# Decode attention over two caches: 64 KB rows per partition, products written over K, fewer buffers

## The chip, the cores and the metric

One core of one Trainium2 chip. The metric is device time in microseconds (us), the median of several executions.

The words used for the units of the core: VectorE (DVE in the profile), TensorE (PE), ScalarE (ACT), SyncE (SP, which here only issues transfers), and the 16 DMA engines, which move data from HBM, the chip's main memory, to SBUF, the core's own memory of 128 partitions.

## The reference

Two independent one-token attention layers, A and B, each with 32 heads of width 128. A attends to all 16384 keys of its cache, B to the last 4096.

```python
q = (x @ wq).reshape(B, Sq, Hq, Dh).transpose(0, 2, 1, 3)
# A: k, v = k_cache, v_cache                      (32 heads x 16384 keys x 128)
# B: k, v = k_cache[:, :, Sk - 4096:, :], ...     (32 heads x  4096 keys x 128)
scores = einsum("bhqd,bhkd->bhqk", q, k) * Dh ** -0.5
o = einsum("bhqk,bhkd->bhqd", softmax(scores), v)
out = concat([oA.reshape(B, Sq, Hq * Dh) @ woA, oB.reshape(B, Sq, Hq * Dh) @ woB])
```

K and V that are read: 32 x 16384 x 128 x 2 bytes x 2 for A, a quarter of that for B; with the projections 352.3 MB in all. Each key is used once, so this is a kernel about moving 352 MB.

## The kernel before

A unit is one 4 MB K load and one 4 MB V load: one head of A, or four heads of B. A partition gets one contiguous row of 32 KB. For A, partition p has keys 128p to 128p+127. For B, the four heads are interleaved: partition 4i+g has the i-th row of head g.

```python
def _load_kv(nc, cx, unit, which):
    # ... (pool, tile [P, unit.keys = 128, DH])
    n = len(unit.heads)                                   # 1 for A, 4 for B
    src = view[unit.heads[0] : unit.heads[0] + n].rearrange("g (i l) d -> i g l d", i=P // n)
    cx.o(nc.sync.dma_start(out=t[:, :, :], in_=src[:, 0, :, :] if n == 1 else src))

def _mult(nc, cx, ch):          # chunk of U = 64 keys a partition
    ch.prod = cx.prod_pool.tile([P, U, DH], BF16, tag="prod", name="prod")
    # ... prod = K chunk * q (broadcast)                  VectorE
def _add(nc, cx, ch):
    # ... half = prod[:, :, :64] + prod[:, :, 64:]        VectorE
# _red: TensorE sums half to red; _softmax: VectorE sums red to sc, ScalarE exp
# _pv: TensorE multiplies p and V, accumulating over the four heads of a group
cx.kt_pool = pool("kt", 2); cx.vt_pool = pool("vt", 2)    # two K and two V buffers
```

Where heads are interleaved, the query block holds each partition's own head's q, and exp gets a bias of -1000 on the partitions of the other heads.

The softmax here doesn't subtract the row's maximum and nothing guards it: scores larger than these inputs give would overflow.

Of the kernel before, what the change touches and what calls it, by code (L numbers as in the profile page):

```python
# [10 lines left out]
P = 128  # L11
# [5 lines left out]
G = 4  # L17
U = 64
SCALE = 1.0 / math.sqrt(DH)
# [21 lines left out]
class _Loads:  # L41



    def __init__(self):
        self.todo, self.free = [], {}
# [16 lines left out]
class _Group:  # L63


    def __init__(self, st, i):
        self.st, self.i, self.heads = st, i, list(range(i * G, (i + 1) * G))
        self.acc = self.cs = None


class _Chunk:


    def __init__(self, unit, i):
        self.unit, self.i, self.k0 = unit, i, i * U
        self.last_of_unit = self.k0 + U == unit.keys


class _Unit:
    kt = vt = None  # L80


def _load_x(nc, cx, st):

    D = st.wq.shape[0]
    KC = D // P
    xT = cx.singles.tile([P, KC], BF16, tag=f"xT{st.name}", name=f"xT{st.name}")
    nc.scalar.dma_start(out=xT[:, :], in_=st.x[0, 0, :].rearrange("(p c) -> p c", c=KC))
    R = st.mix
    st.xb = cx.singles.tile([P, KC, R, P], BF16, tag=f"xb{st.name}", name=f"xb{st.name}")  # L90
    if R > 1:
        cx.o(nc.vector.memset(st.xb[:, :, :, :], 0.0))
    for g in range(R):
        for c in range(KC):
            cx.o(nc.vector.tensor_copy(  # L95
                st.xb[:, c, g, :].rearrange("p (i r) -> p r i", r=R)[:, g, :],
                xT[:, c : c + 1].broadcast_to([P, P // R]),
            ))


def _load_wq(nc, cx, st, tag):
    D, N = st.wq.shape
    KC = D // P
    st.wq_tag = tag
    pool = cx.kt_pool if tag == "kt" else cx.vt_pool
    st.wq_t = pool.tile([P, KC, N], BF16, tag=tag, name="wq_t")
    cx.o(nc.sync.dma_start(out=st.wq_t[:, :, :], in_=st.wq.rearrange("(p c) f -> p c f", c=KC)))  # L107


def _q(nc, cx, st):  # L110


    D, N = st.wq.shape
    KC = D // P
    R = st.mix
# [15 lines left out]
    cx.loads.release(st.wq_tag)  # L131


def _load_wo(nc, cx, st, j0, n):


    J = st.wo.shape[0] // P
    if j0 == 0:
        st.wo_t = cx.kt_pool.tile([P, J, st.DN], BF16, tag="kt", name=f"wo{st.name}")
    src = st.wo.rearrange("(p j) f -> p j f", j=J)  # L140
    cx.o(nc.sync.dma_start(out=st.wo_t[:, j0 : j0 + n, :], in_=src[:, j0 : j0 + n, :]))  # L141

# [37 lines left out]
def _red(nc, cx, ch):  # L180
# [3 lines left out]
    for b in range(nb):  # L184
# [11 lines left out]


# [365 lines left out]
```

## Time and profile before

| kernel before | value |
|---|---|
| time | 829.09 us (829.01 to 829.31, 3 runs) |
| DMA queue busy, share of 16 engines' span | 99.1% |
| VectorE / TensorE busy | 71% / 49% |
| bytes read | 352.3 MB, 426 GB/s over the span |

The page of the kernel before: the DMA's share of each of 40 slices of the span in tenths, and the rate in each; the packets; the load queue; the chain of waits, by engine and by line; four groups of instructions (count, busy us, mean ns, idle time before them and what ended it); and the K and V loads (size, median us from issue to landing).

```profile
DMA  9999999999999999999999999999999999999996
GB/s 380 434 430 432 432 432 435 431 432 430 434 429 434 430 431 430 434 431 426 434 432 430 429 431 430 431 432 432 432 430 431 429 431 433 431 433 431 432 423 285
DMA packets 13133, 352.68 MB, mean 426 GB/s; under 512 B 1714, under 2 KB 1716, under 8 KB 2100
...
q1 hardware_dynamic: 12820, 352.33, 99.1%
...
DMA 69%; DVE 20%; issue 10%; SPq 0%; DVEq 0%; PE 0%
DMA kt<-in_A_k_cache_dram 53%; DMA kt<-in_B_k_cache_dram 13%; DVE prod L160 12%; DVE half L172 6%; DMA woB<-in_B_wo_dram 3%; DVE sc L202 2%; SPq L141 0%; DVE recip L266 0%; DVEq L160 0%; PE out L302 0%; SPq L107 0%; DVE rowB L311 0%
...
L160 DVE TENSOR_TENSOR prod<-kt,qallA 128x8192 bf16<-128x8192 bf16 x64 | 283.3, 4426 | 159.8 <-DMA kt<-in_A_k_cache_dram 159.1
L172 DVE TENSOR_TENSOR half<-prod 128x4096 bf16<-128x4096 bf16 x80 | 182.6, 2282 | 0.0
...
L160 DVE TENSOR_TENSOR prod<-kt,qallB 128x8192 bf16<-128x8192 bf16 x16 | 70.8, 4426 | 40.2 <-DMA kt<-in_B_k_cache_dram 39.9
L232 PE MATMUL acc<-vt,pA 128*16 128x512 bf16 x1024 | 87.2, 474 | 2.0 <-DMA vt<-in_A_v_cache_dram 2.0
...
kt<-in_A_k_cache_dram SPq DMA_DIRECT2D x32, 4096.0 KB, 27.0
vt<-in_A_v_cache_dram SPq DMA_DIRECT2D x32, 4096.0 KB, 29.6
kt<-in_B_k_cache_dram SPq DMA_DIRECT2D x8, 4096.0 KB, 27.0
vt<-in_B_v_cache_dram SPq DMA_DIRECT2D x8, 4096.0 KB, 29.6
```

Two windows of the kernel before (busy us of each engine, then the granted clock, the DMA's share and its rate).

```profile
core 0: us, PE busy (x) PEld busy (x) DVE busy (x) ACT busy (x) POOL busy (x), PEclk, DMA share, GB/s
160.55:199.41 38.86, 17.04 (x96) 5.43 (x96) 28.91 (x13) 1.40 (x8) 0.00 (x0) 0.69 1.00 431
199.41:238.27 38.86, 20.14 (x124) 7.31 (x124) 28.96 (x14) 5.10 (x23) 0.00 (x0) 0.69 1.01 432
```

Read together: the load queue hardly pauses (busy 99.1%), a 4 MB load that needs 9.7 us at 432 GB/s lands 27 to 30 us after its issue, so it queues behind two others, and VectorE works 29 of each 38.9 us. The chain names VectorE because it frees the buffers (SP waits 428.9 us in all for the product in L160), but by then other loads are already queued. The trace also has a record of every DMA packet; a row of 32 KB is one packet:

```
row bytes      4096   8192   16384   32768     (kernel before, lowest busy ns of a packet)
busy ns         159    309     611    1213
```

That is 36.75 ns per 1000 bytes (37.6 ns per KB as the row lengths count it, 1024 bytes) and some 9 ns for each packet. The prediction's "36.75 ns per KB" is the first of these. A load ends with 16 records of 4 bytes, its completion records, of 9 ns each (median). The kernel before also has 18 instruction packets of 16 KB, which took 1.02 to 1.10 us where the lowest for that size is 0.61. At three of them (55, 427 and 795 us) the spread between the first and the last completion record of a load rose by 1.1 to 1.5 us, from 0.5 to 4.9 us in all.

### The profile page before, as it was taken

The page shows a single profiled execution, that of the slowest core. Times are in us where ns is not written, and L with a number is a line of the kernel's source. Part 1 is how long each engine was busy: PE and PEld are TensorE (multiplying, and loading weights), DVE is VectorE, ACT ScalarE, POOL GpSimd, SP SyncE. Part 2 cuts the span into 40 slices and gives each one's busy share as a digit, 9 for nine tenths or more (in the row PEclk, how much of TensorE's full clock was granted, in tenths as well). Part 3 has the DMA queues.
Part 4 walks back from the last instruction along what each step waited for, and adds up shares of the span by engine and source line. Part 5 has one row for each costly group of instructions (what it writes and reads, how often), then busy time and mean ns, then how long its engine had stood idle before and what let it go on. Part 6 is the DMA issues. An engine that isn't in the chain of part 4 may idle for free.

```text
span 827.4 us, 5697 instructions
## 1 busy us (share of the span) xinstructions
PE 402.1 (49%) x2368; PEld 139.4 (17%) x2368; DVE 584.8 (71%) x286; ACT 68.2 (8%) x301; POOL 4.6 (1%) x17
## 2 busy tenths in 40 slices
PE   3356434434554535544454445545455345464355
PEld 1112111111211112211121111111112111121123
DVE  2892777777777777766777777777777776777760
ACT  2000011000100001000110001100010000100010
POOL 2000000000000000000000000000000000000000
PEclk9778687666676676776677676666676766766778
DMA  9999999999999999999999999999999999999996
GB/s 380 434 430 432 432 432 435 431 432 430 434 429 434 430 431 430 434 431 426 434 432 430 429 431 430 431 432 432 432 430 431 429 431 433 431 433 431 432 423 285
DMA packets 13133, 352.68 MB, mean 426 GB/s; under 512 B 1714, under 2 KB 1716, under 8 KB 2100
## 3 DMA queue, kind: packets, MB, share of 16 engines
q1 hardware_dynamic: 12820, 352.33, 99.1%
q8 instruction: 18, 0.29, 0.1%
q10 hardware_dynamic: 288, 0.00, 0.0%
q14 instruction: 7, 0.06, 0.0%
HBM read 352.32 MB, written 0.00 MB: 426 GB/s over the span
## 4 chain that ended last, share of the span: by engine, by line
DMA 69%; DVE 20%; issue 10%; SPq 0%; DVEq 0%; PE 0%
DMA kt<-in_A_k_cache_dram 53%; DMA kt<-in_B_k_cache_dram 13%; DVE prod L160 12%; DVE half L172 6%; DMA woB<-in_B_wo_dram 3%; DVE sc L202 2%; SPq L141 0%; DVE recip L266 0%; DVEq L160 0%; PE out L302 0%; SPq L107 0%; DVE rowB L311 0%
## 5 line engine op out<-in xcount | busy, mean ns | idle before, releaser
L185 PE MATMUL red<-half,ident 128*128 128x512 bf16 x640 | 252.4, 566 | 388.7 <-DVE half L172 388.7
L160 DVE TENSOR_TENSOR prod<-kt,qallA 128x8192 bf16<-128x8192 bf16 x64 | 283.3, 4426 | 159.8 <-DMA kt<-in_A_k_cache_dram 159.1
L172 DVE TENSOR_TENSOR half<-prod 128x4096 bf16<-128x4096 bf16 x80 | 182.6, 2282 | 0.0
L185 PEld LDWEIGHTS <-ident 128*128 128x128 bf16 x640 | 81.9, 128 | 534.0 <-issue 506.2
L160 DVE TENSOR_TENSOR prod<-kt,qallB 128x8192 bf16<-128x8192 bf16 x16 | 70.8, 4426 | 40.2 <-DMA kt<-in_B_k_cache_dram 39.9
L232 PE MATMUL acc<-vt,pA 128*16 128x512 bf16 x1024 | 87.2, 474 | 2.0 <-DMA vt<-in_A_v_cache_dram 2.0
L209 ACT ACTIVATE pA<-sc 128x64 bf16<-128x64 f32 x64 | 16.4, 256 | 512.2 <-DVE sc L202 512.2
L202 DVE TENSOR_REDUCE sc<-red 128x64 f32<-128x512 f32 x80 | 54.8, 684 | 3.7 <-PE red L185 3.6
L232 PEld LDWEIGHTS <-pA 128*16 128x16 bf16 x1024 | 22.5, 99 | 72.6 <-issue 65.2
L209 ACT ACTIVATE p_sb<-sc,off 128x64 bf16<-128x64 f32 x64 | 21.5, 336 | 91.4 <-DVE sc L202 91.4
L256 PE MATMUL f_ps<-acc_sb,sel 128*4 128x128 f32 x128 | 16.6, 273 | 10.7 <-ACT acc_sb L243 10.7
L232 PE MATMUL acc<-vt,p_sb 128*16 128x512 bf16 x256 | 21.3, 464 | 0.0
L243 ACT COPY acc_sb<-acc 128x512 f32<-128x512 f32 x16 | 9.4, 586 | 85.6 <-PE acc L232 85.6
L123 PE MATMUL q_ps<-wq_t,xbA 128*128 128x512 bf16 x32 | 8.7, 439 | 13.1 <-DMA wq_t<-in_A_wq_dram 13.1
L256 PEld LDWEIGHTS f_ps<-acc_sb,sel 128*4 128x4 f32 x128 | 9.8, 86 | 14.5 <-ACT acc_sb L243 12.3
L209 ACT ACTIVATION_READ_ACCUMULATOR pA<-sc 128x1 f32 x64 | 11.9, 187 | 0.0
L209 ACT ACTIVATION_READ_ACCUMULATOR p_sb<-sc,off 128x1 f32 x64 | 11.9, 186 | 0.0
L232 PEld LDWEIGHTS <-p_sb 128*16 128x16 bf16 x256 | 5.6, 97 | 16.3 <-issue 14.1
L123 PE MATMUL q_ps<-wq_t,xbB 128*128 128x512 bf16 x32 | 7.2, 378 | 2.0 <-DMA wq_t<-in_B_wq_dram 1.3
L268 ACT ACTIVATE orow<-f_ps,recip 4x128 bf16<-4x128 f32 x16 | 5.7, 358 | 20.5 <-DVE recip L266 20.5
L95 DVE COPY xbB<-xTB 128x32 bf16<-128x32 bf16 x16 | 1.5, 197 | 8.1 <-DMA xTB<-in_B_x_dram 8.1
L266 DVE RECIPROCAL recip<-f_ps 4x1 f32<-4x1 f32 x16 | 2.4, 150 | 5.8 <-PE f_ps L256 5.8
(35 smaller groups left out, 54.8 us busy)
## 6 DMA issues: line engine op xcount, KB each, us to landing
kt<-in_A_k_cache_dram SPq DMA_DIRECT2D x32, 4096.0 KB, 27.0
vt<-in_A_v_cache_dram SPq DMA_DIRECT2D x32, 4096.0 KB, 29.6
kt<-in_B_k_cache_dram SPq DMA_DIRECT2D x8, 4096.0 KB, 27.0
vt<-in_B_v_cache_dram SPq DMA_DIRECT2D x8, 4096.0 KB, 29.6
wq_t<-in_A_wq_dram SPq DMA_DIRECT2D x1, 4096.0 KB, 12.3
wq_t<-in_B_wq_dram SPq DMA_DIRECT2D x1, 4096.0 KB, 24.1
woA<-in_A_wo_dram SPq DMA_DIRECT2D x2, 2048.0 KB, 31.3
woB<-in_B_wo_dram SPq DMA_DIRECT2D x1, 2048.0 KB, 23.8
```

What stands on the lines that cost most here:

```text
L95: cx.o(nc.vector.tensor_copy(st.xb[:, c, g, :].rearrange("p (i r) -> p r i", r=R)[:, g, :], xT[:, c : c + 1].broadcast_to([P, P // R]),))
L123: cx.o(nc.tensor.matmul(q_ps[:, :], lhsT=st.xb[:, c, g, :], rhs=w[:, g, j * (512 // DH) : (j + 1) * (512 // DH), :], start=(g == 0 and c = ...
L160: cx.o(nc.vector.tensor_tensor(out=ch.prod[:, :, :], in0=u.kt[:, ch.k0 : ch.k0 + U, :], in1=q.rearrange("p (o d) -> p o d", o=1).broadcast ...
L172: cx.o(nc.vector.tensor_tensor(out=ch.half[:, :, :], in0=ch.prod[:, :, 0 : DH // 2], in1=ch.prod[:, :, DH // 2 : DH], op=ALU.add,))
L185: cx.o(nc.tensor.matmul(ch.red[:, :, :], lhsT=cx.ident[:, :], rhs=ch.half[:, :, b * W : (b + 1) * W], start=(b == 0), stop=(b == nb - 1),))
L202: cx.o(nc.vector.tensor_reduce(out=sc[:, :], in_=ch.red[:, :, :], axis=AX.X, op=ALU.add))
L209: cx.o(nc.scalar.activation(out=ch.p[:, :, g, :], in_=sc[:, :].rearrange("p (t e) -> p t e", e=4), func=ACT.Exp, scale=SCALE, bias=0.0 if ...
L232: cx.o(nc.tensor.matmul(gr.acc[r : r + 4 * G, :], lhsT=ch.p[:, t, :, :], rhs=u.vt[:, k : k + 4, :], start=(first and t < 4), stop=(last an ...
L243: cx.o(nc.scalar.copy(gr.acc_sb[:, :], gr.acc[:, :]))
L256: cx.o(nc.tensor.matmul(gr.f_ps[:, 0:DH], lhsT=cx.sel[:, e, :], rhs=gr.acc_sb[:, e * DH : (e + 1) * DH], start=False, stop=(e == 3), skip_ ...
L266: cx.o(nc.vector.reciprocal(recip[:, :], gr.f_ps[:, DH : DH + 1]))
L268: cx.o(nc.scalar.activation(out=gr.orow[:, :], in_=gr.f_ps[:, 0:DH], func=ACT.Copy, scale=recip[:, 0:1]))
```

## The change

Its intent: the same bytes in half as many loads with rows twice as long, to lose fewer fixed costs in the stream that bounds the kernel. A unit is now 8 MB of K and 8 MB of V, 64 KB a partition: two heads of A (partition 2i+g) or eight of B (partition 8i+g). To make room, q*k and the half sums are written over K, there are two K buffers and one V buffer, and each unit has its own accumulator.

```diff
-G = 4
+KEYS = 256
 def _load_kv(...):
-    n = len(unit.heads)
-    src = view[unit.heads[0] : unit.heads[0] + n].rearrange("g (i l) d -> i g l d", i=P // n)
-    cx.o(nc.sync.dma_start(out=t[:, :, :], in_=src[:, 0, :, :] if n == 1 else src))
+    src = view[unit.h0 : unit.h0 + unit.R].rearrange("g (i l) d -> i g l d", l=KEYS)
+    cx.o(nc.sync.dma_start(out=t[:, :, :], in_=src))          # R = 2 for A, 8 for B
 def _mult(...):
-        out=ch.prod[:, :, :], in0=u.kt[:, ch.k0 : ch.k0 + U, :],
+        out=k, in0=k,                                          # k = the K chunk itself
 def _add(...):
-        out=ch.half[:, :, :], in0=ch.prod[:, :, 0:64], in1=ch.prod[:, :, 64:128],
+        out=k[:, :, 0:64], in0=k[:, :, 0:64], in1=k[:, :, 64:128],
-    cx.vt_pool = pool("vt", 2)
+    cx.vt_pool = pool("vt", 1)
     # ... (P.V of a whole unit in one go, during the next unit; projections first;
     #      the last V goes to a K buffer; cut)
```

The shape in which a load names its source, slowest dimension first:

```
             before                      changed
A    128 rows x 32 KB             64 x 2 rows x 64 KB
B    32 x 4 rows x 32 KB          16 x 8 rows x 64 KB
```

More of the change, by code (lines that the diff above doesn't have):

```diff
@@ L41, with __init__ @@
 class _Loads:
-    def __init__(self):
-        self.todo, self.free = [], {}
+    def __init__(self, free):
+        self.todo, self.free = [], free
     def add(self, pool, fn):
@@ L60, in pump @@
             fn()
-class _Group:
-    def __init__(self, st, i):
-        self.st, self.i, self.heads = st, i, list(range(i * G, (i + 1) * G))
-        self.acc = self.cs = None
 class _Chunk:
@@ L75, in __init__, with _load_x, _load_wq @@
         self.unit, self.i, self.k0 = unit, i, i * U
-        self.last_of_unit = self.k0 + U == unit.keys
 class _Unit:
-    kt = vt = None
-def _load_x(nc, cx, st):
+    def __init__(self, st, i):
+        self.st, self.i, self.R = st, i, st.R
+        self.h0 = i * st.R
+        self.chunks = [_Chunk(self, c) for c in range(KEYS // U)]
+        self.stage = None
+def _load_x(nc, cx, st, at):
     D = st.wq.shape[0]
     KC = D // P
+    R = st.R
     xT = cx.singles.tile([P, KC], BF16, tag=f"xT{st.name}", name=f"xT{st.name}")
     nc.scalar.dma_start(out=xT[:, :], in_=st.x[0, 0, :].rearrange("(p c) -> p c", c=KC))
-    R = st.mix
-    st.xb = cx.singles.tile([P, KC, R, P], BF16, tag=f"xb{st.name}", name=f"xb{st.name}")
-    if R > 1:
-        cx.o(nc.vector.memset(st.xb[:, :, :, :], 0.0))
+    n = KC * R * P
+    st.xb = cx.scr[:, at : at + n].rearrange("p (c g m) -> p c g m", c=KC, g=R)
+    cx.o(nc.vector.memset(cx.scr[:, at : at + n], 0.0))
     for g in range(R):
-        for c in range(KC):
-            cx.o(nc.vector.tensor_copy(
-                st.xb[:, c, g, :].rearrange("p (i r) -> p r i", r=R)[:, g, :],
-                xT[:, c : c + 1].broadcast_to([P, P // R]),
-            ))
-def _load_wq(nc, cx, st, tag):
+        cx.o(nc.vector.tensor_copy(
+            st.xb[:, :, g, :].rearrange("p c (i r) -> p r c i", r=R)[:, g, :, :],
+            xT[:, :].rearrange("p (c o) -> p c o", o=1).broadcast_to([P, KC, P // R]),
+        ))
+    return at + n
+def _load_wq(nc, cx, st, w):
     D, N = st.wq.shape
     KC = D // P
-    st.wq_tag = tag
-    pool = cx.kt_pool if tag == "kt" else cx.vt_pool
-    st.wq_t = pool.tile([P, KC, N], BF16, tag=tag, name="wq_t")
-    cx.o(nc.sync.dma_start(out=st.wq_t[:, :, :], in_=st.wq.rearrange("(p c) f -> p c f", c=KC)))
+    if w == 0:
+        cx.wq_t = cx.vt_pool.tile([P, 2, KC, N], BF16, tag="vt", name="wq_t")
+    st.wq_t = cx.wq_t[:, w, :, :]
+    cx.o(nc.sync.dma_start(out=st.wq_t, in_=st.wq.rearrange("(p c) f -> p c f", c=KC)))
 def _q(nc, cx, st):
@@ L114, in _q @@
     KC = D // P
-    R = st.mix
+    R = st.R
     n = N // R
@@ L130, in _q, with _load_kv @@
         cx.o(nc.scalar.copy(st.qall[:, j * 512 : (j + 1) * 512], q_ps[:, :]))
-    cx.loads.release(st.wq_tag)
 def _load_wo(nc, cx, st, j0, n):
     J = st.wo.shape[0] // P
-    if j0 == 0:
-        st.wo_t = cx.kt_pool.tile([P, J, st.DN], BF16, tag="kt", name=f"wo{st.name}")
+    if cx.wo_t is None:
+        cx.wo_t = cx.vt_pool.tile([P, 2, J, st.DN], BF16, tag="vt", name="wo_t")
     src = st.wo.rearrange("(p j) f -> p j f", j=J)
+    st.wo_t = cx.wo_t[:, st.at // st.DN, :, :]
     cx.o(nc.sync.dma_start(out=st.wo_t[:, j0 : j0 + n, :], in_=src[:, j0 : j0 + n, :]))
-def _load_kv(nc, cx, unit, which):
-    pool, tag = (cx.kt_pool, "kt") if which == "k" else (cx.vt_pool, "vt")
-    t = pool.tile([P, unit.keys, DH], BF16, tag=tag, name=tag)
-    setattr(unit, tag, t)
+def _load_kv(nc, cx, unit, which, tag):
+    pool = cx.kt_pool if tag == "kt" else cx.vt_pool
+    t = pool.tile([P, KEYS, DH], BF16, tag=tag, name=which)
+    setattr(unit, which, t)
+    unit.v_tag = tag
     st = unit.st
-    view = st.k_view if which == "k" else st.v_view
-    n = len(unit.heads)
-    src = view[unit.heads[0] : unit.heads[0] + n].rearrange("g (i l) d -> i g l d", i=P // n)
-    cx.o(nc.sync.dma_start(out=t[:, :, :], in_=src[:, 0, :, :] if n == 1 else src))
+    view = st.k_view if which == "kt" else st.v_view
+    src = view[unit.h0 : unit.h0 + unit.R].rearrange("g (i l) d -> i g l d", l=KEYS)
+    cx.o(nc.sync.dma_start(out=t[:, :, :], in_=src))
 def _mult(nc, cx, ch):
     u = ch.unit
-    ch.prod = cx.prod_pool.tile([P, U, DH], BF16, tag="prod", name="prod")
-    q = u.st.qall[:, u.q_at * DH : (u.q_at + 1) * DH]
+    k = u.kt[:, ch.k0 : ch.k0 + U, :]
+    q = u.st.qall[:, u.i * DH : (u.i + 1) * DH]
     cx.o(nc.vector.tensor_tensor(
-        out=ch.prod[:, :, :],
-        in0=u.kt[:, ch.k0 : ch.k0 + U, :],
+        out=k, in0=k,
         in1=q.rearrange("p (o d) -> p o d", o=1).broadcast_to([P, U, DH]),
@@ L165, in _mult @@
     ))
-    if ch.last_of_unit:
-        cx.loads.release("kt")
 def _add(nc, cx, ch):
-    ch.half = cx.half_pool.tile([P, U, DH // 2], BF16, tag="half", name="half")
+    k = ch.unit.kt[:, ch.k0 : ch.k0 + U, :]
     cx.o(nc.vector.tensor_tensor(
-        out=ch.half[:, :, :],
-        in0=ch.prod[:, :, 0 : DH // 2],
-        in1=ch.prod[:, :, DH // 2 : DH],
-        op=ALU.add,
+        out=k[:, :, 0 : DH // 2], in0=k[:, :, 0 : DH // 2], in1=k[:, :, DH // 2 : DH], op=ALU.add,
     ))
@@ L187, in _red @@
             lhsT=cx.ident[:, :],
-            rhs=ch.half[:, :, b * W : (b + 1) * W],
+            rhs=ch.unit.kt[:, ch.k0 : ch.k0 + U, b * W : (b + 1) * W],
             start=(b == 0),
@@ L191, in _red @@
         ))
+    if ch.k0 + U == KEYS:
+        cx.loads.release("kt")
 def _softmax(nc, cx, ch):
-    u, gr = ch.unit, ch.unit.group
-    if gr.cs is None:
-        gr.cs = cx.cs_pool.tile([P, 2, G], F32, tag=f"cs{gr.st.name}", name="cs")
-    sc = cx.small.tile([P, U], F32, tag="sc", name="sc")
-    cx.o(nc.vector.tensor_reduce(out=sc[:, :], in_=ch.red[:, :, :], axis=AX.X, op=ALU.add))
-    if len(u.heads) == 1:
-        ch.p = cx.pA[u.heads[0] % G][ch.i]
-    else:
-        ch.p = cx.p_pool.tile([P, U // 4, G, 4], BF16, tag="p", name="p_sb")
-    for h in u.heads:
-        g = h % G
+    u = ch.unit
+    R = u.R
+    if ch.i == 0:
+        u.cs = cx.cs_pool.tile([P, KEYS // U, R], F32, tag=f"cs{u.st.name}", name="cs")
+    sc = cx.sc_pool.tile([P, U], F32, tag="sc", name="sc")
+    cx.o(nc.vector.tensor_reduce(out=sc[:, :], in_=ch.red[:, :, :], axis=AX.X, op=ALU.add))
+    ch.p = u.st.p_pool.tile([P, U // 4, R, 4], BF16, tag=f"p{u.st.name}", name="p_sb")
+    for g in range(R):
         cx.o(nc.scalar.activation(
@@ L213, in _softmax @@
             scale=SCALE,
-            bias=0.0 if len(u.heads) == 1 else cx.off[:, g : g + 1],
-            accum_out=gr.cs[:, ch.i, g : g + 1],
-        ))
-def _pv(nc, cx, ch):
-    u, gr = ch.unit, ch.unit.group
-    first = u.heads[0] == gr.heads[0] and ch.i == 0
-    last = u.heads[-1] == gr.heads[-1] and ch.last_of_unit
-    if first:
-        cx.turn = 1 - cx.turn
-        gr.acc = cx.acc[cx.turn]
-    T = U // 4
+            bias=u.st.off[:, g : g + 1],
+            accum_out=u.cs[:, ch.i, g : g + 1],
+        ))
@@ L229, in _pv @@
+def _pv(nc, cx, u):
+    R = u.R
+    u.csum = cx.small.tile([P, R], F32, tag=f"csum{u.st.name}", name="csum")
+    cx.o(nc.vector.tensor_reduce(
+        out=u.csum[:, :], in_=u.cs[:, :, :].rearrange("p i g -> p g i"), axis=AX.X, op=ALU.add,
+    ))
+    cx.turn = 1 - cx.turn
+    acc = cx.acc[cx.turn]
+    T = KEYS // 4
     for t in range(T):
         r = 32 * (t % 4)
-        k = ch.k0 + 4 * t
+        ch = u.chunks[4 * t // U]
         cx.o(nc.tensor.matmul(
-            gr.acc[r : r + 4 * G, :],
-            lhsT=ch.p[:, t, :, :],
-            rhs=u.vt[:, k : k + 4, :],
-            start=(first and t < 4),
-            stop=(last and t >= T - 4),
-        ))
@@ L239, in _pv @@
-    if ch.last_of_unit:
-        cx.loads.release("vt")
-    if last:
-        gr.acc_sb = cx.accs_pool.tile([P, 4 * DH], F32, tag="accs", name="acc_sb")
-        cx.o(nc.scalar.copy(gr.acc_sb[:, :], gr.acc[:, :]))
-    return gr if last else None
-def _fin_fold(nc, cx, gr):
-    gr.f_ps = cx.psf_pool.tile([G, DH + 1], F32, tag="f", name="f_ps")
-    for i in range(2):
-        cx.o(nc.tensor.matmul(
-            gr.f_ps[:, DH : DH + 1], lhsT=gr.cs[:, i, :], rhs=cx.ones_col[:, 0:1],
-            start=(i == 0), stop=(i == 1), skip_group_check=True,
-        ))
+            acc[r : r + 4 * R, :],
@@ new lines, in _pv, with _fin_fold @@
+            lhsT=ch.p[:, t % (U // 4), :, :],
+            rhs=u.vt[:, 4 * t : 4 * t + 4, :],
+            start=(t < 4),
+            stop=(t >= T - 4),
+        ))
+    cx.loads.release(u.v_tag)
+    u.acc_sb = cx.accs_pool.tile([P, 4 * DH], F32, tag="accs", name="acc_sb")
+    cx.o(nc.scalar.copy(u.acc_sb[:, :], acc[:, :]))
+def _fin_fold(nc, cx, u):
+    R = u.R
+    u.f_ps = cx.psf_pool.tile([8, DH + 1], F32, tag="f", name="f_ps")
+    cx.o(nc.tensor.matmul(
+        u.f_ps[0:R, DH : DH + 1], lhsT=u.csum[:, :], rhs=cx.ones_col[:, 0:1],
+        start=True, stop=True, skip_group_check=True,
+    ))
@@ L255, in _fin_fold, with _fin_row @@
     for e in range(4):
         cx.o(nc.tensor.matmul(
-            gr.f_ps[:, 0:DH],
-            lhsT=cx.sel[:, e, :],
-            rhs=gr.acc_sb[:, e * DH : (e + 1) * DH],
+            u.f_ps[0:R, 0:DH],
+            lhsT=cx.sel[:, e, 0:R],
+            rhs=u.acc_sb[:, e * DH : (e + 1) * DH],
             start=False, stop=(e == 3), skip_group_check=True,
         ))
-def _fin_row(nc, cx, gr):
-    recip = cx.small.tile([G, 1], F32, tag="recip", name="recip")
-    cx.o(nc.vector.reciprocal(recip[:, :], gr.f_ps[:, DH : DH + 1]))
-    gr.orow = cx.small.tile([G, DH], BF16, tag="orow", name="orow")
+def _fin_row(nc, cx, u):
+    R = u.R
+    recip = cx.small.tile([8, 1], F32, tag="recip", name="recip")
+    cx.o(nc.vector.reciprocal(recip[0:R, :], u.f_ps[0:R, DH : DH + 1]))
+    u.orow = cx.small.tile([8, DH], BF16, tag="orow", name="orow")
@@ L268, in _fin_row, with _fin_col @@
     cx.o(nc.scalar.activation(
-        out=gr.orow[:, :], in_=gr.f_ps[:, 0:DH], func=ACT.Copy, scale=recip[:, 0:1]
+        out=u.orow[0:R, :], in_=u.f_ps[0:R, 0:DH], func=ACT.Copy, scale=recip[0:R, 0:1]
     ))
-def _fin_col(nc, cx, gr):
-    st = gr.st
+def _fin_col(nc, cx, u):
+    st = u.st
     J = st.wo.shape[0] // P
-    R = DH // J
-    at = (len(st.groups) - 1 - gr.i) * G * R
-    for r in range(R):
+    n = DH // J
+    last = u.i == len(st.units) - 1
+    for r in range(n):
+        at = cx.place_at - n * u.h0 - r
@@ L281, in _fin_col @@
         cx.o(nc.tensor.matmul(
             cx.oc_ps[:, st.oc_at : st.oc_at + J],
-            lhsT=cx.place[0:G, r, at : at + P],
-            rhs=gr.orow[:, r * J : (r + 1) * J],
-            start=(cx.oc_first and r == 0), stop=(gr.i == len(st.groups) - 1 and r == R - 1),
+            lhsT=cx.place[0 : u.R, at : at + P],
+            rhs=u.orow[0 : u.R, r * J : (r + 1) * J],
+            start=(cx.oc_first and r == 0), stop=(last and r == n - 1),
             skip_group_check=True,
@@ L309, in _out @@
     if j0 + n == J:
-        row = cx.singles.tile([1, st.DN], BF16, tag=f"row{st.name}", name=f"row{st.name}")
+        row = cx.accs_pool.tile([1, st.DN], BF16, tag="accs", name=f"row{st.name}")
         cx.o(nc.vector.tensor_copy(row[0:1, 0:w], out[0]))
@@ L342 @@
     cx.singles = pool("singles", 1)
-    cx.small = pool("small", 4)
+    cx.small = pool("small", 1)
     cx.kt_pool = pool("kt", 2)
-    cx.vt_pool = pool("vt", 2)
-    cx.prod_pool = pool("prod", 1)
-    cx.half_pool = pool("half", 2)
-    cx.accs_pool = pool("accs", 2)
+    cx.vt_pool = pool("vt", 1)
+    cx.accs_pool = pool("accs", 1)
     cx.cs_pool = pool("cs", 2)
-    cx.p_pool = pool("p", 4)
+    cx.sc_pool = pool("sc", 2)
+    cx.p_poolA = pool("pA", 8)
+    cx.p_poolB = pool("pB", 4)
     cx.red_pool = pool("red", 2, **PS)
@@ L354, with problem @@
     cx.psout_pool = pool("psout", 1, **PS)
-    ld = cx.loads = _Loads()
-    ld.free = {"kt": 2, "vt": 2}
+    ld = cx.loads = _Loads({"kt": 1, "vt": 1})
+    cx.scr = cx.kt_pool.tile([P, KEYS * DH], BF16, tag="kt", name="scr")
+    cx.wo_t = None
+    def problem(name, x, k_cache, v_cache, wq, wo, sk0, W, at):
+        st = _Problem()
+        st.name, st.x, st.wq, st.wo, st.at = name, x, wq, wo, at
+        st.R = P * KEYS // W
+        st.DN = wo.shape[1]
+        st.k_view = k_cache[0, :, sk0 : sk0 + W, :]
+        st.v_view = v_cache[0, :, sk0 : sk0 + W, :]
+        st.oc_at, st.out_rows = (0, (0, 32)) if name == "A" else (64, (64, 96))
+        st.p_pool = cx.p_poolA if name == "A" else cx.p_poolB
+        st.units = [_Unit(st, i) for i in range(k_cache.shape[1] // st.R)]
+        return st
+    stA = problem("A", A_x, A_k_cache, A_v_cache, A_wq, A_wo, 0, SkA, 0)
+    stB = problem("B", B_x, B_k_cache, B_v_cache, B_wq, B_wo, SkB - WB, WB, A_wo.shape[1])
+    units = []
+    per = len(stA.units) // len(stB.units)
+    for i, u in enumerate(stA.units):
+        units.append(u)
+        if i % per == per - 1:
+            units.append(stB.units[i // per])
+    n = len(units)
+    ld.add("vt", lambda: _load_wq(nc, cx, stA, 0))
+    ld.add(None, lambda: _load_wq(nc, cx, stB, 1))
+    for i, u in enumerate(units):
+        ld.add("kt", lambda u=u: _load_kv(nc, cx, u, "kt", "kt"))
+        if i:
+            ld.add("vt", lambda u=units[i - 1]: _load_kv(nc, cx, u, "vt", "vt"))
+    ld.add("kt", lambda u=units[-1]: _load_kv(nc, cx, u, "vt", "kt"))
+    J = A_wo.shape[0] // P
+    pieces = [(stA, 0, J // 2), (stA, J // 2, J // 2)]
+    j0 = 0
+    for x in (J // 2, J // 4, J // 8, J // 16, J // 16):
+        pieces.append((stB, j0, x))
+        j0 += x
+    for i, p in enumerate(pieces):
+        ld.add(None if i else "vt", lambda p=p: _load_wo(nc, cx, *p))
+    ld.pump()
+    at = _load_x(nc, cx, stA, 0)
+    at = _load_x(nc, cx, stB, at)
     cx.ones_col = cx.singles.tile([P, 1], F32, tag="ones_col", name="ones_col")
     nc.gpsimd.memset(cx.ones_col[:, :], 1.0)
-    ones_mat = cx.singles.tile([P, P], BF16, tag="ones_mat", name="ones_mat")
-    nc.gpsimd.memset(ones_mat[:, :], 1.0)
+    ones = cx.scr[:, at : at + 2 * P]
+    nc.gpsimd.memset(ones, 1.0)
     cx.ident = cx.singles.tile([P, P], BF16, tag="ident", name="ident")
@@ L364 @@
         out=cx.ident[:, :],
-        in_=ones_mat[:, :],
+        in_=ones[:, 0:P],
         pattern=[[-1, P]],
@@ L371 @@
     )
-    cx.sel = cx.singles.tile([P, 4, G], F32, tag="sel", name="sel")
+    n_r = DH // J
+    cx.place_at = n_r * (stA.units[-1].h0) + n_r - 1
+    w = cx.place_at + P
+    cx.place = cx.singles.tile([8, 2 * P], BF16, tag="place", name="place")
+    nc.gpsimd.affine_select(
+        out=cx.place[:, 0:w],
+        in_=ones[0:8, 0:w],
+        pattern=[[1, w]],
+        compare_op=ALU.is_equal,
+        fill=0.0,
+        base=-cx.place_at,
+        channel_multiplier=-n_r,
+    )
+    cx.sel = cx.singles.tile([P, 4, 8], F32, tag="sel", name="sel")
     nc.vector.tensor_reduce(
         out=cx.sel[:, :, :].rearrange("p e g -> p g e"),
-        in_=cx.ident[:, :].rearrange("p (t g e) -> p g e t", t=4, g=8)[:, 0:G, :, :],
+        in_=cx.ident[:, :].rearrange("p (t g e) -> p g e t", t=4, g=8),
         axis=AX.X,
@@ L381 @@
     )
-    cx.off = cx.singles.tile([P, G], F32, tag="off", name="off")
-    nc.vector.tensor_reduce(
-        out=cx.off[:, :],
-        in_=cx.ident[:, :].rearrange("p (i g) -> p g i", g=G),
-        axis=AX.X,
-        op=ALU.add,
-    )
-    nc.vector.tensor_scalar(
-        out=cx.off[:, :], in0=cx.off[:, :], scalar1=-1.0, scalar2=1000.0,
-        op0=ALU.add, op1=ALU.mult,
-    )
-    J = A_wo.shape[0] // P
-    R = DH // J
-    w = 2 * P - G * R
-    ones_row = cx.singles.tile([G, R * w], BF16, tag="ones_row", name="ones_row")
-    nc.gpsimd.memset(ones_row[:, :], 1.0)
-    cx.place = cx.singles.tile([G, R, w], BF16, tag="place", name="place")
-    nc.gpsimd.affine_select(
-        out=cx.place[:, :, :],
-        in_=ones_row[:, :].rearrange("p (r c) -> p r c", r=R),
-        pattern=[[-1, R], [1, w]],
-        compare_op=ALU.is_equal,
-        fill=0.0,
-        base=-(P - G * R),
-        channel_multiplier=-R,
-    )
-    cx.pA = []
-    for g in range(G):
-        cx.pA.append([])
-        for i in range(2):
-            t = cx.singles.tile([P, U // 4, G, 4], BF16, tag=f"pA{g}{i}", name=f"pA{g}{i}")
-            nc.gpsimd.memset(t[:, :, :, :], 0.0)
-            cx.pA[g].append(t)
+    for st in (stA, stB):
+        st.off = cx.singles.tile([P, st.R], F32, tag=f"off{st.name}", name=f"off{st.name}")
+        nc.vector.tensor_reduce(
+            out=st.off[:, :],
+            in_=cx.ident[:, :].rearrange("p (i g) -> p g i", g=st.R),
+            axis=AX.X,
+            op=ALU.add,
+        )
+        nc.vector.tensor_scalar(
+            out=st.off[:, :], in0=st.off[:, :], scalar1=-1.0, scalar2=1000.0,
+            op0=ALU.add, op1=ALU.mult,
+        )
     cx.turn = 0
@@ L427 @@
     ]
-    def problem(name, x, k_cache, v_cache, wq, wo, sk0, W, at):
-        st = _Problem()
-        st.name, st.x, st.wq, st.wo, st.W, st.at = name, x, wq, wo, W, at
-        st.H = k_cache.shape[1]
-        st.DN = wo.shape[1]
-        st.k_view = k_cache[0, :, sk0 : sk0 + W, :]
-        st.v_view = v_cache[0, :, sk0 : sk0 + W, :]
-        st.oc_at, st.out_rows = (0, (0, 32)) if name == "A" else (64, (64, 96))
-        st.mix = 1 if W == SkA else G
-        st.groups = [_Group(st, i) for i in range(st.H // G)]
-        return st
@@ L441 @@
-    stA = problem("A", A_x, A_k_cache, A_v_cache, A_wq, A_wo, 0, SkA, 0)
-    stB = problem("B", B_x, B_k_cache, B_v_cache, B_wq, B_wo, SkB - WB, WB, A_wo.shape[1])
-    units = []
-    for h in range(stA.H):
-        units.append((stA, [h]))
-        if h % G == G - 1:
-            units.append((stB, list(range(h - G + 1, h + 1))))
-    chunks = []
-    for i, (st, heads) in enumerate(units):
-        u = units[i] = _Unit()
-        u.st, u.heads, u.group = st, heads, st.groups[heads[0] // G]
-        u.keys = st.W * len(heads) // P
-        u.q_at = heads[0] // len(heads)
-        u.chunks = [_Chunk(u, i) for i in range(u.keys // U)]
-        chunks += u.chunks
@@ L460 @@
-    ld.add("vt", lambda: _load_wq(nc, cx, stA, "vt"))
-    n = len(units)
-    for i in range(n + 1):
-        if i == G - 1:
-            ld.add("kt", lambda: _load_wq(nc, cx, stB, "kt"))
-        if i < n:
-            ld.add("kt", lambda u=units[i]: _load_kv(nc, cx, u, "k"))
-        if i:
-            ld.add("vt", lambda u=units[i - 1]: _load_kv(nc, cx, u, "v"))
-    pieces = [(stA, 0, J // 2), (stA, J // 2, J // 2)]
-    j0 = 0
-    for x in (J // 2, J // 4, J // 8, J // 16, J // 16):
-        pieces.append((stB, j0, x))
-        j0 += x
@@ L474 @@
-    for p in pieces:
-        ld.add(None if p[1] else "kt", lambda p=p: _load_wo(nc, cx, *p))
-    _load_x(nc, cx, stA)
-    _load_x(nc, cx, stB)
-    ld.pump()
     _q(nc, cx, stA)
+    _q(nc, cx, stB)
+    ld.release("kt")
+    ld.release("vt")
     fins = []
     def fin_pe():
-        for gr in fins:
-            if gr.stage == 0:
-                _fin_fold(nc, cx, gr)
-                gr.stage = 1
-            elif gr.stage == 2:
-                _fin_col(nc, cx, gr)
-                gr.stage = 9
-        fins[:] = [gr for gr in fins if gr.stage != 9]
@@ L494, in fin_dve @@
-    def fin_dve():
-        for gr in fins:
-            if gr.stage == 1:
-                _fin_row(nc, cx, gr)
-                gr.stage = 2
-    def pv(ch):
-        gr = _pv(nc, cx, ch)
-        if gr is not None:
-            gr.stage = 0
-            fins.append(gr)
-    prev = None
-    waiting = []
-    for c, ch in enumerate(chunks):
-        if c == 2 * (G - 1):
-            _q(nc, cx, stB)
-        _mult(nc, cx, ch)
-        if prev is not None:
-            _softmax(nc, cx, prev)
-            waiting.append(prev)
-        fin_pe()
-        _add(nc, cx, ch)
-        fin_dve()
-        _red(nc, cx, ch)
-        if len(waiting) > 1:
-            pv(waiting.pop(0))
-        prev = ch
@@ L522 @@
-    _softmax(nc, cx, prev)
-    waiting.append(prev)
-    for ch in waiting:
-        fin_pe()
-        fin_dve()
-        pv(ch)
+        for u in fins:
+            if u.stage == 0:
+                _fin_fold(nc, cx, u)
+                u.stage = 1
+            elif u.stage == 2:
+                _fin_col(nc, cx, u)
+                u.stage = 9
+        fins[:] = [u for u in fins if u.stage != 9]
+    def fin_dve():
+        for u in fins:
+            if u.stage == 1:
+                _fin_row(nc, cx, u)
+                u.stage = 2
@@ new lines, in pv @@
+    def pv(u):
+        _pv(nc, cx, u)
+        u.stage = 0
+        fins.append(u)
+    prev = None
+    for i, u in enumerate(units):
+        for ch in u.chunks:
+            _mult(nc, cx, ch)
+            if prev is not None:
+                _softmax(nc, cx, prev)
+            fin_pe()
+            _add(nc, cx, ch)
+            fin_dve()
+            _red(nc, cx, ch)
+            if i and ch.i == min(i - 1, 2):
+                pv(units[i - 1])
+            prev = ch
+    _softmax(nc, cx, prev)
@@ L528 @@
+    fin_pe()
+    fin_dve()
+    pv(units[-1])
     while fins:
```

## The prediction

> **What bounds it now.** The DMA queue. The page shows the load queue busy 99.1% of 16 engines' span; steady windows of 38.86 us move 430 to 432 GB/s[...]. VectorE is busy 71%, TensorE 49%. The chain of waits is 69% DMA; its VectorE pieces only say when a buffer came free. The issue list shows 27 to 30 us from issue to landing for loads that need 9.7 us: two are always queued behind the running one. The 352.3 MB stay.
>
> [...] The DMA packet records give busy time by size: 4 KB 159 ns, 8 KB 309, 16 KB 611, 32 KB 1213 (lowest values; the 32 KB mean is 1218). That is a line: 36.75 ns per KB plus about 9 ns. Each completion record of a load[...] takes another 9 ns. The rest is outside the stream: 2.8 us before the first row, 18 instruction fetches of 16 KB on the same engines, which let the slowest engine lag the fastest by 0.5 us early, 3.4 later, 4.9 near the end, and 3 us after the last landing.
>
> **What the change removes.** K/V rows grow from 32 to 64 KB: 640 row packets an engine become 320, saving 320 x 9 ns = 2.9 us (estimate from the line above); 80 K/V loads become 40, saving 0.4 us of completion records. All of it is on the critical path. Sum 3.2 us, if a 64 KB row stays one packet. [...] no trace here shows it yet. If rows are cut in two, only 0.4 us is left.
>
> **What it adds or moves.** In-place multiply and add have the same shapes (4.43 and 2.28 us); score sums 0.68. A unit of four chunks needs 4 x 7.4 = 29.5 us of VectorE against 38.9 us for its 16.8 MB. Exps grow on ScalarE (for B about 4.2 us a chunk), far from limiting. With one V buffer, the next V is issued after the previous unit's P.V: K lands at t, three chunks 22 us, reduction 3.5, 64 P.V matmuls 4.2 to 5.5 us (16 took 1.04 to 1.09): t+31, against t+38.9 when the queue would run dry: slack 8 us. K is released near t+36, needed at t+58. First compute begins at 41 us instead of 23, costless because V and wo follow the last K anyway. Projections end by 32 us, before K0 lands. Tail: 10 us of wo-A covers the last P.V and fold.
>
> **Prediction.** 826.1 us; 80% range 824.4 to 829.3. Faster by over 2%: 0.01; within 2%: 0.96; slower: 0.03.
>
> **What would show it.** About 5120 row packets of 65,536 B at about 2420 ns, no idle stretch in the DMA slices, 432 to 434 GB/s, landing to landing of K about 38.7 us; SP's wait for P.V ending 7 us or more before the running K load lands; tail unchanged; VectorE instruction times unchanged.
>
> **What would make it wrong.** 64 KB rows cut in two (about 828.7); instruction fetches falling on one engine (up to 1.5 us each); the V slack vanishing because P.V or VectorE slows, idling the queue each unit (20 us per us of shortfall); a late K1; strided in-place operands slowing VectorE over 30%.

The forecast's sum: 320 x 9 ns for row packets and 40 x 9 ns for completion records, 3.2 us. Where the second paragraph has 2.8 us before the first row, the packet records have the first 16 rows start 2.0 to 2.9 us into the span.

## The result, and the profile after

| | before | changed |
|---|---|---|
| time, us | 829.12 (4 runs) | 1052.85 (1045.08 to 1054.47, 4 runs) |
| ratio | | 1.268, 95% interval 1.264 to 1.272 |
| DMA rate over the span, GB/s | 426 | 335 |
| VectorE busy, us | 584.8 | 584.2 |

A ratio is the mean time of one kernel's runs over that of the other's of the same rounds, so not quite the ratio of the medians. The changed kernel is 27% slower where 0.4% faster was predicted.

The page of the changed kernel, the same parts as before:

```profile
DMA  9999999999999999999999999997999999999970
GB/s 399 439 437 439 435 429 208 282 437 214 267 437 430 434 434 227 252 435 244 242 420 424 410 429 287 203 421 260 202 344 405 404 437 399 200 299 244 193 286 32
DMA packets 7375, 352.70 MB, mean 335 GB/s; under 512 B 1074, under 2 KB 1076, under 8 KB 1460
...
q1 hardware_dynamic: 7060, 352.33, 95.7%
...
DMA 33%; another core or an unknown queue 23%; DVE 23%; PE 14%; issue 7%; ACT 1%; SPq 0%; ACTq 0%; DVEq 0%
DMA kt<-in_A_k_cache_dram 21%; DVE kt L151 11%; DVE kt L160 9%; DMA vt<-in_A_v_cache_dram 7%; PE acc L214 7%; PE red L170 5%; DMA wo_t<-in_B_wo_dram 5%; DVE sc L188 3%; PE f_ps L234 1%; ACT acc_sb L223 1%; PE out L279 0%; DVE recip L245 0%; SPq L132 0%; SPq L101 0%
...
L151 DVE TENSOR_TENSOR kt<-kt,qallA 128x8192 bf16<-128x8192 bf16 x64 | 282.8, 4419 | 147.8 <-DMA kt<-in_A_k_cache_dram 147.8
L160 DVE TENSOR_TENSOR kt<-kt 128x4096 bf16<-128x4096 bf16 x80 | 182.6, 2283 | 0.0
...
L151 DVE TENSOR_TENSOR kt<-kt,qallB 128x8192 bf16<-128x8192 bf16 x16 | 70.7, 4421 | 129.2 <-DMA kt<-in_B_k_cache_dram 129.2
L214 PE MATMUL acc<-vt,p_sb 128*8 128x512 bf16 (+1 forms) x1280 | 97.2, 471 | 98.8 <-DMA vt<-in_B_v_cache_dram 75.6
```

Its K and V loads, from the view of DMA issues (8 MB each):

```profile
kt<-in_A_k_cache_dram SPq DMA_DIRECT2D x16, 47.6
vt<-in_A_v_cache_dram SPq DMA_DIRECT2D x16, 36.7
kt<-in_B_k_cache_dram SPq DMA_DIRECT2D x4, 74.8
vt<-in_B_v_cache_dram SPq DMA_DIRECT2D x4, 56.2
```

Windows of the changed kernel (columns as before):

```profile
core 0: us, PE busy (x) PEld busy (x) DVE busy (x) ACT busy (x) POOL busy (x), PEclk, DMA share, GB/s
120.00:140.00 20.00, 12.92 (x95) 4.76 (x94) 11.24 (x7) 2.38 (x10) 0.00 (x0) 0.67 0.98 421
140.00:160.00 20.00, 7.22 (x17) 2.36 (x17) 19.27 (x9) 1.55 (x8) 0.00 (x0) 0.58 1.09 416
160.00:180.00 20.00, 10.89 (x94) 4.20 (x93) 9.59 (x7) 2.38 (x10) 0.00 (x0) 0.76 1.01 211
180.00:200.00 20.00, 0.00 (x0) 0.00 (x0) 0.00 (x0) 0.00 (x0) 0.00 (x0) 0.50 0.95 210
...
1020.00:1050.00 30.00, 15.44 (x206) 9.09 (x205) 1.28 (x5) 1.67 (x4) 0.00 (x0) 0.76 0.10 36
```

What to see here. First, VectorE's instructions last what they did before (4419 and 2283 ns against 4426 and 2282): work in place cost nothing here. Secondly, the DMA row is nearly all nines, as before, while the rate falls in whole stretches to about 200 GB/s. In the windows from 160 to 200 us the engines are busy (share 1.01 and 0.95) at 211 and 210 GB/s: they do not wait for anything to be issued, they move data at half speed. A busy share alone hides this; the rate beside it shows it. Thirdly, the slow stretches are B's loads: the load that starts near 160 us is the first of B, and the median from issue to landing is 75 us for B's K against 48 for A's. (In the chain, "another core or an unknown queue" stands where the profile could not name the releaser; the group lines show VectorE's waits there as waits for K loads.) Fourthly, from 1020 us to nearly the end the DMA share is 0.10, which is 1.6 of 16 engines: most have finished, and the kernel waits for a few.

The packet records show the two speeds. All 5120 K/V rows are single packets of 65,536 bytes, as predicted:

```
rows of 64 KB, changed kernel      ns
lowest / median                  2415 / 2422
rows up to 2600                  3803 of 5120
rows over 4600                   1035 of them (B has 1024 rows); median of the slow rows about 5090
```

So three quarters of the rows take the predicted time, about as many rows as B has take 2.1 times that, and some 280 lie between.

### The profile page after: what moved, and what is told of

Read it like the earlier page. It is cut to its first block, busy times and chain, and to the rows that moved or that the text cites. A ratio compares the mean times of both kernels' runs of the same rounds, so it can differ in the third digit from the quotient of the medians.

```text
span 1051.4 us, 5921 instructions
## 1 busy us (share of the span) xinstructions
PE 393.8 (37%) x2392; PEld 149.7 (14%) x2392; DVE 584.2 (56%) x303; ACT 114.9 (11%) x560; POOL 1.2 (0%) x8
## 3 DMA queue, kind: packets, MB, share of 16 engines
q1 hardware_dynamic: 7060, 352.33, 95.7%
## 4 chain that ended last, share of the span: by engine, by line
DMA 33%; another core or an unknown queue 23%; DVE 23%; PE 14%; issue 7%; ACT 1%; SPq 0%; ACTq 0%; DVEq 0%
DMA kt<-in_A_k_cache_dram 21%; DVE kt L151 11%; DVE kt L160 9%; DMA vt<-in_A_v_cache_dram 7%; PE acc L214 7%; PE red L170 5%; DMA wo_t<-in_B_wo_dram 5%; DVE sc L188 3%; PE f_ps L234 1%; ACT acc_sb L223 1%; PE out L279 0%; DVE recip L245 0%; SPq L132 0%; SPq L101 0%
## 5 line engine op out<-in xcount | busy, mean ns | idle before, releaser
L170 PE MATMUL red<-kt,ident 128*128 128x512 bf16 x640 | 249.5, 560 | 523.6 <-DVE kt L160 523.6
L151 DVE TENSOR_TENSOR kt<-kt,qallA 128x8192 bf16<-128x8192 bf16 x64 | 282.8, 4419 | 147.8 <-DMA kt<-in_A_k_cache_dram 147.8
L160 DVE TENSOR_TENSOR kt<-kt 128x4096 bf16<-128x4096 bf16 x80 | 182.6, 2283 | 0.0
L151 DVE TENSOR_TENSOR kt<-kt,qallB 128x8192 bf16<-128x8192 bf16 x16 | 70.7, 4421 | 129.2 <-DMA kt<-in_B_k_cache_dram 129.2
L214 PE MATMUL acc<-vt,p_sb 128*8 128x512 bf16 (+1 forms) x1280 | 97.2, 471 | 98.8 <-DMA vt<-in_B_v_cache_dram 75.6
L191 ACT ACTIVATE p_sb<-sc,offA 128x64 bf16<-128x64 f32 x128 | 43.5, 341 | 511.6 <-DVE sc L188 511.6
L214 PEld LDWEIGHTS <-p_sb 128*8 128x8 bf16 (+1 forms) x1280 | 36.8, 105 | 164.6 <-issue 145.6
L191 ACT ACTIVATE p_sb<-sc,offB 128x64 bf16<-128x64 f32 x128 | 42.7, 335 | 93.8 <-DVE sc L188 93.8
L191 ACT ACTIVATION_READ_ACCUMULATOR p_sb<-sc,offB 128x1 f32 x128 | 24.0, 188 | 0.0
L191 ACT ACTIVATION_READ_ACCUMULATOR p_sb<-sc,offA 128x1 f32 x128 | 24.0, 187 | 0.0
```

The costliest lines, as they stand in the source:

```text
L151: cx.o(nc.vector.tensor_tensor(out=k, in0=k, in1=q.rearrange("p (o d) -> p o d", o=1).broadcast_to([P, U, DH]), op=ALU.mult,))
L160: cx.o(nc.vector.tensor_tensor(out=k[:, :, 0 : DH // 2], in0=k[:, :, 0 : DH // 2], in1=k[:, :, DH // 2 : DH], op=ALU.add,))
L170: cx.o(nc.tensor.matmul(ch.red[:, :, :], lhsT=cx.ident[:, :], rhs=ch.unit.kt[:, ch.k0 : ch.k0 + U, b * W : (b + 1) * W], start=(b == 0), s ...
L191: cx.o(nc.scalar.activation(out=ch.p[:, :, g, :], in_=sc[:, :].rearrange("p (t e) -> p t e", e=4), func=ACT.Exp, scale=SCALE, bias=u.st.of ...
L214: cx.o(nc.tensor.matmul(acc[r : r + 4 * R, :], lhsT=ch.p[:, t % (U // 4), :, :], rhs=u.vt[:, 4 * t : 4 * t + 4, :], start=(t < 4), stop=(t ...
```

## The experiments

Theory W (write side). What slows B's rows is the shape of the load and with it the partitions to which the rows go that are written at the same time. By it, with 16 as the source's slowest dimension these writes hold each other up (B's rows in the changed kernel: 5.09 us); with 32 or more in front they do not (32 x 4 in the kernel before: median 1215 ns for half the bytes; A's 64 x 2 in the changed kernel: most rows at about 2.42 us). How rows are dealt out to the engines, and which partitions are in each other's way, no trace or run shows. Two results are suppositions, to be tested: rows at 5.1 us for 16 x 2, as measured for 16 x 8, and 4 x 2.42 = 9.7 us for 16 x 1.

Rivals: H, something else about B's units is slow (64 KB rows, 8 MB loads, the lone V buffer, work in place); and A, the HBM addresses collide, because heads lie exactly 4 MB apart and rows 64 KB.

### e1_same_bytes_128 and e2_near_16x8: one pattern against another over nearly the same bytes

```diff
 # e1: B's loads only (wrong result on purpose)
-    src = view[...].rearrange("g (i l) d -> i g l d", l=KEYS)        # 16 x 8 rows
+    src = rows64k[128 * unit.i : 128 * unit.i + 128, :]              # 128 rows
 # e2: B's loads only (wrong result on purpose); skips every ninth row
+    src = rows64k[128 * unit.i : 128 * unit.i + 144, :].rearrange("(i a) f -> i a f", a=9)[:, 0:8, :]
```

> The changed kernel with only B's K and V loads altered: 128 contiguous rows of 64 KB, so that the source pattern is two-dimensional (128 x 65,536 B) and not 16 x 8 x 65,536 B. Same bytes, same row length, same partitions; the result is wrong on purpose. Theory W (write side): [...] this run has every 64 KB row at about 2.42 us and takes 826 us, as first predicted. Rival H (64 KB rows, one V buffer or in-place work make B units slow): stays at about 1050 us. Rival A (HBM addresses at large power-of-two distances collide): fast too only if contiguous rows avoid the collision; told apart by the next run.

> The pair of the first run: nearly the same bytes (16 groups of 8 contiguous 64 KB rows, one row skipped after each group), but the pattern is 16 x 8 x 65,536 B again. Wrong result on purpose. [...] Theory W: as slow as the changed kernel, 1030 to 1070 us, B rows at 5.1 us. Rival A (address distances): fast, about 826 us. Rival H: slow as well.

Measured: e1 took 825.9 us (825.82 to 826.46), ratio 0.9962 (0.9946 to 0.9979) to the kernel before; no 64 KB row took over 3.1 us. e2 took 1052.15 us (a single look), and its 1038 rows over 4600 ns have a median of 5086 ns, as in the changed kernel. The page of e1, then two of its windows:

```profile
DMA  9999999999999999999999999999999999999996
GB/s 382 433 458 408 455 420 440 439 427 445 417 448 417 446 420 443 423 442 437 427 436 427 433 430 433 437 429 440 423 443 423 443 420 445 421 445 417 448 405 290
DMA packets 7375, 352.70 MB, mean 428 GB/s; under 512 B 1074, under 2 KB 1076, under 8 KB 1460
```

```profile
160.00:180.00 20.00, 10.24 (x94) 4.10 (x94) 10.14 (x7) 2.12 (x10) 0.00 (x0) 0.76 1.00 433
180.00:200.00 20.00, 6.60 (x16) 2.27 (x16) 20.00 (x9) 5.08 (x29) 0.00 (x0) 0.67 0.98 426
```

The rate line of e2:

```profile
GB/s 399 439 437 439 435 425 210 284 437 210 270 432 430 437 427 232 247 430 260 232 418 429 417 407 304 213 414 300 202 314 437 400 432 372 210 299 265 150 300 31
```

Where the changed kernel had 211 and 210 GB/s, e1 has 433 and 426, with the same DMA share; e2 has the same dips as the changed kernel. What follows: the shape in which B's loads name their rows is the cause of the whole loss. It is not the row length, the load size, the buffers or the work in place, which e1 shares with the changed kernel. It is not the distance between addresses either: e2 reads groups of eight neighbouring rows, 576 KB from group to group, which is no power of two, and is as slow.

### e6_16x8_32k: the pattern with short rows

```diff
+        for a in range(2):      # B only: two loads of 4 MB, each half of every row
+            dma_start(out=t[:, a * 128 : (a + 1) * 128, :], in_=src[:, :, a * 128 : (a + 1) * 128, :])
```

> B's 8 MB loads cut into two loads of 4 MB, each 16 x 8 rows of 32 KB (half of every row): the row length and load size of the kernel before, the pattern of the changed kernel; result right. Theory W: still slow, rows of 32 KB at about 2.55 us instead of 1.21, total 1030 to 1070 us. A rival that blames 64 KB rows or 8 MB loads: fast, about 828 us.

Measured: 1055.91 us (a single look), result correct; most 32 KB rows took about 2.5 us instead of 1.21. The row length and load size of the kernel before do not help; the pattern alone hurts.

### e5_b_by_head and e10_b_by_pair: fewer partitions a load

```diff
 # e5: B's load as 8 loads of 1 MB                 # e10: as 4 loads of 2 MB
+    for g in range(8):                            +    for g in range(4):
+        dma_start(t[16*g : 16*g+16], head g)      +        dma_start(t[32*g : 32*g+32], heads 2g, 2g+1)
```

> B's 8 MB loads cut into 8 loads of 1 MB, one a head, each to 16 neighbouring partitions[...]. Wrong result on purpose. Theory W: [...] a row takes about 4 x 2.42 = 9.7 us where the engines run in step; 8 loads of 8 rows at 9.7 against 5.1 us add about 290 us: 1250 to 1400 us (less if engines drift apart). Rival A and a rival that blames the 16 x 8 pattern itself[...]: fast, 826 to 840 us.

> B's 8 MB loads cut into 4 loads of 2 MB, each two heads (16 x 2 rows of 64 KB) to 32 neighbouring partitions (result: order of heads in the partitions is not what the compute expects, wrong on purpose). Theory W: [...] rows at 5.1 us and 1030 to 1070 us. A rival by which cutting into smaller loads on few partitions is what cost in the by-head run (1231 us with 1 MB loads): between the 1231 of 8 loads and the 1053 of one, about 1110 to 1180 us.

Measured: e5 1231.49 us, e10 1031.02 us. The rate line of e5:

```profile
GB/s 409 443 418 434 442 160 117 301 342 136 192 427 434 433 294 130 177 431 149 145 370 427 435 410 163 207 429 161 160 410 401 440 377 104 131 237 160 112 197 130
```

| B's load goes to | row, us, as theory W had it | slow rows, median (highest), us | us |
|---|---|---|---|
| 128 partitions, 128 rows (e1) | 2.42 | none (3.1) | 825.9 |
| 128 partitions, 16 x 8 | 5.1 | 5.1 (7.4) | 1052.85 |
| 32 partitions, 16 x 2 (e10) | 5.1 | 5.1 (6.9) | 1031.0 |
| 16 partitions, 16 x 1 (e5) | 9.7 | 7.6 (9.4) | 1231.5 |

The rival of small loads on few partitions expected 1110 to 1180 us for e10 and is out: a load to 32 partitions in this shape is no slower than one to 128. Theory W's order is right in all four lines, of which the second was known when the theory was made. e5 fell a little short of what I had written (1250 us at least): most of its slow rows lie between 7 and 9.4 us and not at 9.7. Why, was not shown.

One comparison in this table bears on reading against writing. e5 and the changed kernel name the same source rows with 16 in front. They differ in the partitions that row e of head g goes to (16g+e instead of 8e+g) and in the number of loads, and four loads in e10 were no slower than one. Yet the slow rows take 7.6 us in one and 5.1 in the other, so the destination counts. What it is about the destination was not shown: the packet records name neither engine nor partition, and no run kept 16 in front with all 128 partitions in another order, which would have been the direct test.

### e7_slow_k_only and e8_slow_v_only: half the dose

```diff
 # B's K loads (e7) or V loads (e8) keep 16 x 8; the other is 128 rows, as in e1 (wrong data on purpose)
```

> Half the dose: B's K loads keep the 16 x 8 pattern, B's V loads are 128 contiguous rows (wrong result on purpose). Rows alone: 4 loads x 8 rows x (5.09 - 2.42) us = 85 us above 826, so 911; with half of the unexplained rest (about 55 us of drift between engines) 940. Theory W: 911 to 940. If the lone V buffer turns slow V loads into extra stalls, this run is clearly under the V-only one.

> The other half: B's V loads keep the 16 x 8 pattern, B's K loads are 128 contiguous rows (wrong result on purpose). Theory W: 911 to 940 again. If the lone V buffer adds stalls of its own, 10 us or more above the K-only run.

Measured: 926.24 us with slow K, 921.77 us with slow V, which is 100 and 96 us above e1. With one of the two streams slow, the lone V buffer adds no stalls that show: slow V loads are, if anything, the cheaper ones. But 100 + 96 = 196 us is less than the 227 us (1052.85 - 825.9) of both together. The packet records of these runs say where the rest lies. Against e1, the busy time of an engine rose by 93 us in e7 and by 95 us in e8, and by 190 us with both; its idle time rose by 7 and 1 us, but by 37 us with both. So the slowed rows add up, and what does not is idle time of the DMA engines, discussed below. Whether more buffers would have shortened it was not tried.

(e8 passed as a correct result although B's keys were wrong. With these inputs the softmax weights are almost equal, so the check of results hardly sees K. See the last experiment.)

### e9_all_32k_rows: is the 3 us of e1 the packet cost?

```diff
+    for a in range(2):      # every K/V load in two halves of 32 KB rows; B as 128 rows (wrong on purpose)
```

> As the run with 128 contiguous rows for B (wrong result on purpose), but every 8 MB load cut into two loads of half rows (32 KB): the changed kernel's compute, buffers and order with the kernel before's row length and load size. If the gain of the 128-row run is the per-packet cost (9 ns a row, as the prediction's sum has it), it goes: 829.1 us, 828.7 to 829.6. If it came from buffers, in-place work or order: stays at 825.9.

Measured: 828.96 us (828.91 to 829.14), ratio 0.9998 (0.9985 to 1.0011). With 32 KB rows the gain is gone, and all else of the change is worth nothing either way. The 3.2 us that the prediction expected are the cost of packets and load completions.

### f1_b_32x4: a version that beats both

A keeps its 64 KB rows. B's 8 MB buffer is filled by two loads in the kernel before's shape, 32 x 4 rows of 32 KB, four heads in each half; the query block, the biases and exp go by four heads, with zeros kept in p and in the sums for the other four.

```diff
+    L = KEYS * st.M // unit.R                     # M = 2 for A, 4 for B: heads in one load
+    for a in range(unit.R // st.M):
+        h = unit.h0 + a * st.M
+        src = view[h : h + st.M].rearrange("g (i l) d -> i g l d", l=L)
+        cx.o(nc.sync.dma_start(out=t[:, a * L : (a + 1) * L, :], in_=src))
-    for g in range(R):
+    for g in range(ch.a * M, (ch.a + 1) * M):     # exp of this chunk's own four heads
-    cx.p_poolA = pool("pA", 8)
+    cx.p_poolA = pool("pA", 6)                    # room for the larger query block
```

> A mend with right results: A keeps 8 MB loads of 64 KB rows; B's 8 MB buffer is filled by two loads of 4 MB, each 32 x 4 rows of 32 KB (the kernel before's pattern), four heads in each half of the buffer. Theory W[...]: no slow row; A's 256 row packets an engine saved are worth 256 x 9 ns = 2.3 us, 32 fewer load completions 0.3 us: 826.5 us, range 825.8 to 827.3. Rival H (something else of the B units): above 900 us.

Measured: 826.57 us (826.53 to 827.05), correct, ratio 0.997 (0.9956 to 0.9983). Its page:

```profile
DMA  9999999999999999999999999999999999999996
GB/s 381 438 451 423 438 430 432 429 436 446 411 453 417 442 426 438 430 430 434 418 446 426 438 426 438 426 426 443 436 418 449 427 436 429 433 421 438 424 424 284
DMA packets 8526, 352.69 MB, mean 427 GB/s; under 512 B 1202, under 2 KB 1204, under 8 KB 1588
```

No dip is left. It is 0.3% faster than the kernel before, too little to count as faster at 2%, and 226 us faster than the changed kernel.

### c1_after_scaled and c2_f1_scaled: are the results right?

```diff
-SCALE = 1.0 / math.sqrt(DH)
+SCALE = 4000.0 / math.sqrt(DH)     # in the changed kernel (c1) and in f1 (c2)
```

> A check of results, not of time: the changed kernel with the softmax scale times 4000 (wrong on purpose), because with the true scale the weights are almost equal and a run with wrong B keys passed as correct. Time 1045 to 1055 us; its relative error is the number to match.

> The mended kernel (B in 32 x 4 rows) with the softmax scale times 4000. If its B keys, heads and masks are matched rightly, its relative error equals that of the changed kernel with the same scale to three digits or so; if not, it differs plainly. Time about 826.6 us.

Measured: relative errors 0.35305840 and 0.35305837, times 1046.28 and 826.83 us. The mended kernel computes the same as the changed one where the keys do matter. This compares the two with each other, not with the reference at that scale.

## Why the prediction was wrong

Point by point:

- *"The DMA queue" bounds the kernel*: right, before and after (busy 99.1% and 95.7%).
- *VectorE instruction times unchanged*: right (4419 and 2283 ns).
- *A 64 KB row stays one packet, "5120 row packets of 65,536 B at about 2420 ns"*: right for their number and for most of A's rows (median of all rows 2422 ns), wrong for B's 1024 rows.
- *"Sum 3.2 us"*: right as a cost of packets. e1 gained 3.2 us (829.07 to 825.9), and e9 lost it again with 32 KB rows. The predicted 826.1 us is e1's time to 0.2 us.
- *The V slack*: in e1, the run in which nothing else disturbs it, the V load in the middle of the kernel is issued at 519.9 us while the running K load lands at 528.9 us. That is 9 us early (8 predicted), and K loads land 38.7 us apart, as predicted.
- *The step that failed*: "36.75 ns per KB plus about 9 ns", taken as the time of any packet. It held only for loads with 32 or more in front (32 x 4 and 128 rows of 32 KB: median 1215 ns, none over 2.0 us; 64 x 2 rows of 64 KB: most at about 2.42 us; 128 rows of 64 KB: none over 3.1 us). The prediction costed how long each row is and never asked in what shape a load names its rows and to which partitions they go. B went from 32 x 4 to 16 x 8 rows, and with 16 in front its rows took 5.09 us instead of 2.42. Of the prediction's list of what would make it wrong, none named this; it looked for starved queues, and in the first slow stretch (160 to 200 us, DMA share 1.01 and 0.95) the engines were hardly short of work.

Where the time went, against e1 (spans 1051.4 and 824.2 us, a difference of 227 us): busy time of packets, averaged over the 16 engines, rose from 817.6 to 1008.0 us, which is 190 us. B's own rows, 64 an engine on average, make 64 x (5.09 - 2.42) = 171 us of that; the other 20 us are mostly A's rows slowed, it seems where some engines are still in B's load (in e6, where size tells A's rows from B's, A's took 24 us an engine more than in e1). The remaining 37 us are idle engines, 21 of them in the last 30 us of the kernel and the rest after 500 us. The spread between the first and the last of a load's 16 completion records grows from 0.5 to 4.9 us in the kernel before. In the changed kernel it grows with B's loads, to between 14 and 21 us from 490 us on and 36 us at 989 us, shrinks to about 8 us between some of them, and is 30.7 us on the very last load (4.9 us before): this is the stretch with a DMA share of 0.10. My reading of these spreads is that B's loads do not slow all engines alike, so that some fall behind and the others run out of issued loads before these catch up. Why particular engines lose, the records cannot tell. This part is an account from the traces; the half-dose runs only show that the idle time grows faster than the dose.

## What to carry to other kernels

A load that covers 128 partitions in large rows can still run at half speed: look at the slowest dimension of its source, not only at sizes. Here 16 in front, with eight partitions to each, halved the rate (210 and 211 GB/s), and 32, 64 and 128 in front kept it (32 x 4: 430 to 432 GB/s; 128 rows: 426 and 433; 64 x 2: most rows at about 2.42 us). Read the DMA's rate beside its busy share: from 160 to 180 us the share was 1.01 at 211 GB/s in the changed kernel and 1.00 at 433 in e1. And when a change re-interleaves data to make rows longer, ask about the shape of the load as well as the packets, or try the load pattern alone first.
